# Splitting the first chunk's sixteen weight blocks into twelve and four around the second chunk, in a fused attention and two-layer expert kernel

## The chip, the cores and the metric

One core of one Trainium2 chip runs the whole kernel as one launch. The metric is device time in microseconds. Three runs of the kernel before took 1052.74, 1054.63 and 1058.1 us; their median, 1054.63 us, is the time before. One further execution was recorded by the hardware profiler: it took 1055.97 us, of which 1054.2 us are the span that the profile shows.

## What is computed

The reference has three stages. `a` is 4 numbers, `b` is 2.

```python
# 1: attention over windows: 32 queries against 8 memory rows and 56 context rows
scores = scale * q_c @ k_full.T
a = exp(scores - scores.max(-1)); a = a / (a.sum(-1) + 1e-9)
x = (a @ v_full), laid out as (3072, 512)
# 2: two dense layers with a rational function between them
h = x @ w_in                                   # (3072, 2048)
g = (a[0] + a[1]*h + a[2]*h**2 + a[3]*h**3) / (1 + |b[0]|*|h| + |b[1]|*h**2 + 1e-6)
x = g @ w_out                                  # (3072, 512)
# 3: each token goes to the best of 8 experts, 512 -> 1024 -> 512 with relu between
```

`w_in` and `w_out` arrive as 64-bit floats. TensorE gets no such numbers, so each weight is rebuilt on the chip as a 32-bit float and cut into a high and a low part; each product in stage 2 is three matmuls (high by high, high by low, low by high).

## The kernel before, in words

The 3072 tokens are 24 groups of 128 (attention) and 8 chunks of three groups (stage 2). The 2048 inner columns are 16 weight blocks of 128. Everything is written out by hand, in program order, on in-order queues: TensorE (PE), VectorE (DVE), ScalarE (ACT), GpSimd (POOL) and the DMA queue of SyncE (SP). A stall of one instruction holds back all that stands behind it on its engine.

**The loop** (L1031) has one step n for each pair of chunk and weight block, chunk by chunk: `i, f = divmod(n, 16)`. Step n issues the first product of pair n (`mm1`, L379: 12 matmuls into one of two banks), the elementwise work of pair n-1 on DVE (`el_t` L399 and L395, `el_g` L413 to L415), the cut of pair n-2 (`split`, L422 and L423), and the second product of pair n-3 (`mm2`, L430, L431, L434: 9 matmuls into three accumulator banks). After the sixteenth `mm2` of a chunk, `evac` copies the three banks to SBUF. Around this, lists name for each step what else runs: attention steps (scores L233, `at_pt` L284, values L297, `at_xt` L316), and the routing of a finished chunk (`rt_steps`, seven chunks inside the loop).

**DVE operations from outside** the elementwise work go to a list `side`; `weave` puts one of them behind each of the five elementwise operations, and the rest at the end of the step.

**Weights.** The 32 pieces (16 blocks of each matrix, 512 KB each) are converted while the first chunk runs. A piece is a load on SP's queue into a raw buffer (L608), three DVE operations (L625, L628, L631, the last being the last to read the raw buffer), a cast on ACT (L619) and a subtraction on POOL (L620). Raw buffers, or slots, are used in turn by three pieces. A freed slot is loaded again at the start of the next step. Four pieces are converted ahead of the loop; `RATE` says how many each step converts, two in most of steps 0 to 15.

**Ahead of the loop** the string `SEQ` orders the first three attention groups: `l` loads, `a` scores, `p` and `v` and `x` the rest, `f` empties `side`, `c3` does three conversion operations, `w` starts a load.

**Groups 3 to 8.** `ATT0` gives the steps of groups 3 to 5. Groups 3 and 5 have a buffer for all keys and values; groups 4 and 6 to 8 load keys and values in halves into one buffer each (six steps, with a load between the halves); from group `G2`, 9, two buffers each are used.

**Three PSUM banks** (`XB`) serve attention and routing. `ban` keeps one for the reciprocal of the rational function up to step `NP` and one as the converter's scratch.

`late_consts` (L973) loads the gate weights and a mask at step 17: POOL clears a tile, SP loads it and the mask, and DVE casts the mask (L977).

Of the kernel before, what the change touches and what calls it, by code (L numbers as in the profile page):

```python
# [18 lines left out]
D = 512  # L19
# [22 lines left out]
@with_exitstack  # L42
def build(ctx: ExitStack, tc, q, k, v, w_in, w_out, a, b, w_gate, w1, w2, cst, out):
# [64 lines left out]
    XX = [XX0, XX1]  # L108
    sxh = [cut(xx0, 1024 * i, 512, (4, 128)) for i in range(2)]
    sxl = [cut(xx0, 1024 * i + 512, 512, (4, 128)) for i in range(2)]  # L110
    hh_ = [cut(xx0, 2048, 1024, (8, 128)), cut(xx1, 1024, 1024, (8, 128))]
    hl_ = [cut(xx1, 0, 1024, (8, 128)), cut(xx1, 2048, 1024, (8, 128))]
    WOb = []
# [46 lines left out]
    def kbuf(g, j):  # L160
        return KV[0][:, 0, j] if g in (1, 3, 5) else ks[j] if g < 3 else k2[j] if g >= G2 else kbd

    def vbuf(g, j):
        return KV[0][:, 1, j] if g in (1, 3, 5) else vs[j] if g < 3 else v2[j] if g >= G2 else vbd

# [3 lines left out]
    def xbuf(g):  # L169
        return xsb if g < 3 else pmb[0] if g < 6 else pmb[1]  # L170

# [13 lines left out]
    def ld_all(g, m, eng=nc.sync):  # L185
        src, buf = ((k, kbuf), (v, vbuf))[m]
        if g in (1, 3, 5):
# [38 lines left out]
    def at_score(g, j):  # L226
# [83 lines left out]
    def at_xt(g):  # L310
# [6 lines left out]
        sl = slice(128 * r, 128 * r + 128)  # L317
        xh, xl = XX[i % 2][:, 0, :, sl], XX[i % 2][:, 1, :, sl]
        nc.scalar.copy(out=xh, in_=pt)
# [8 lines left out]
    def attn_steps(g):  # L328
        def score(j):
            at_score(g, j)  # L330
            if j == 1:
                ld_next(g + 1, ld_k)
                if 4 < g + 1 < 24:
                    ld_q(g + 1)
# [5 lines left out]

        if g in (3, 5):
            def scores():
                score(0)
                score(1)
                if g == 3:
                    ld_q(4)
                    ld_all(5, 0)

            def values():
                pv(0)  # L350
                pv(1)
                if g == 3:
                    ld_all(5, 1)

# [18 lines left out]
    def mm1(n):  # L373
        i, f = divmod(n, 16)
        h = HB[n % 2][:, 0:384]
        m = 0
        for kk in range(4):
            for w, x in ((0, 0), (0, 1), (1, 0)):
                nc.tensor.matmul(  # L379
                    h, lhsT=WI[:, f, w, 128 * kk:128 * kk + 128], rhs=XX[i % 2][:, x, kk, :],  # L380
                    start=(m == 0), stop=(m == 11),
# [43 lines left out]
    def mm2(n):  # L425
        f = n % 16
        gh, gl = GG[:, n % 2, 0], GG[:, n % 2, 1]
        for r in range(3):
            sl = slice(128 * r, 128 * r + 128)
            nc.tensor.matmul(ACC[r], lhsT=gh[:, sl], rhs=wo(f, 0), start=(f == 0), stop=False)  # L430
            nc.tensor.matmul(ACC[r], lhsT=gh[:, sl], rhs=wo(f, 1), start=False, stop=False)  # L431
        for r in range(3):
            sl = slice(128 * r, 128 * r + 128)
            nc.tensor.matmul(ACC[r], lhsT=gl[:, sl], rhs=wo(f, 0), start=False, stop=(f == 15))  # L434

    def evac(i):
        for r in range(3):
            if r == 1:
                nc.vector.tensor_copy(out=X2[:, r, 0:D], in_=ACC[r])
            else:  # L440
                nc.scalar.copy(out=X2[:, r, 0:D], in_=ACC[r])

# [9 lines left out]
    def rt_t(i, r, pb, x2t):  # L452
        pt = pb.rearrange("p (a k) -> p a k", a=4)
        for kk in range(4):
            nc.tensor.transpose(pt[:, kk], X2[:, r, 128 * kk:128 * kk + 128], ident)
        nc.scalar.copy(out=x2t, in_=pb)
# [60 lines left out]
    def rt_cols(i):  # L517
        vt = nc.vector
        ch(lambda: vt.tensor_reduce(out=r_gt, in_=r_ex, op=ALU.add, axis=AX.X))
        ch(lambda: vt.tensor_scalar(out=r_gt, in0=r_gt, scalar1=1e-9, scalar2=None, op0=ALU.add))  # L520
        ch(lambda: vt.reciprocal(out=X2[:, :, D:D + 1], in_=r_gt.unsqueeze(2)))

        def toks():
            for r in range(3):
                nc.gpsimd.tensor_scalar(
                    out=X2[:, r, D + 1:D + 2].bitcast(I32), in0=jcol,
                    scalar1=float(128 * (3 * i + r)), scalar2=None, op0=ALU.add,
# [6 lines left out]
    def rt_store(i, r):  # L534
        x = nc.gpsimd.indirect_dma_start(
            out=xs_d,
            out_offset=bass.IndirectOffsetOnAxis(ap=r_di[:, r:r + 1], axis=0),
            in_=X2[:, r],
            in_offset=None,
# [51 lines left out]
    def slot(m):  # L591
        return m if m < 3 else (0, 3, 4)[m % 3]

# [304 lines left out]
    def w_conv():  # L898
        m = done[0]
        if m < len(order):  # L900
            ops, tail = order[m][1](tmp1, scratch[0])
            side.extend(ops)
# [88 lines left out]
    for g in range(23, 2, -1):  # L991
        base = 16 * (g // 3 - 1) + 5 * (g % 3) - (1 if g < G2 else 0)
        for k_, (o, x) in enumerate(attn_steps(g)):
            if g < 6:
                (at if g == 4 and k_ == 1 else at_)(ATT0[g - 3][k_], x)
            else:
                (at_ if g == 6 and not k_ else at)(base + o, x)
    for i in range(NCH - 1):
        for o, x in rt_steps(i):
            at(16 * (i + 1) + 5 + o, x)  # L1000

    for t in (k2[1], v2[1]):
# [252 lines left out]
```

## Time and profile before

| what | value |
|---|---|
| median of three runs | 1054.63 us (1052.74 to 1058.1) |
| profiled execution | 1055.97 us |
| its span | 1054.2 us |
| PE busy | 994.7 us, 94% |
| DVE busy | 691.2 us, 66% |
| ACT busy | 623.5 us, 59% |
| POOL busy | 381.5 us, 36% |

Busy times count an engine's own work. PE's matmuls are pipelined and their ends are modelled, so 94% is no measure of the peak; what counts below is where PE had nothing to run. A timeline row gives start, length, engine, line, operation, what it writes and reads, and in brackets how long the engine had been idle before it and what ended that. The clock column (PEclk) is the granted clock of TensorE as a share of its upper level.

### The profile page before, as it was taken

The numbers are of one execution on the slowest core, as the hardware profiler recorded it, in microseconds if no ns is written. First come the engines' busy times: TensorE is split into PE (matmuls) and PEld (weight loads), VectorE is DVE, ScalarE is ACT, GpSimd is POOL, SyncE is SP. The second block draws the span as 40 slices with busy tenths as digits, with TensorE's granted clock in tenths as the row PEclk, the third lists the DMA queues.
The fourth block names the chain that finished last, engine by engine and source line by source line (L and its number), as shares of the span: only waits on it lengthen the run. The fifth ranks groups of instructions, "written<-read, shape, count | busy, mean of one in ns | idle before, by whom it ended". The sixth has DMA issues, their size and how long they took to land. (4 is left out here: it accounts for less than half of the span.)

```text
span 1054.2 us, 18765 instructions
## 1 busy us (share of the span) xinstructions
PE 994.7 (94%) x6427; PEld 851.1 (81%) x6427; DVE 691.2 (66%) x1276; ACT 623.5 (59%) x1178; POOL 381.5 (36%) x412
## 2 busy tenths in 40 slices
PE   4678879999999999999999999998999999999996
PEld 3566668888888888888888888886888888888885
DVE  5799877767787787787787788967423424344421
ACT  2577567767777777777777778865423324234321
POOL 2367554453363464464464464541100000000010
PEclk9699899999999999999999999999999999999999
DMA  9755422341121121121121022022115133144311
GB/s 245 209 183 167 144 61 71 91 120 52 51 81 51 51 81 51 51 80 51 52 81 51 21 101 70 1 71 70 43 43 198 35 111 131 51 165 156 112 41 38
DMA packets 48460, 93.10 MB, mean 88 GB/s; under 512 B 6999, under 2 KB 15455, under 8 KB 48352
## 3 DMA queue, kind: packets, MB, share of 16 engines
q1 hardware_dynamic: 43520, 78.52, 24.5%
q0 software_dynamic: 4080, 12.61, 3.2%
q8 instruction: 53, 0.87, 0.3%
q10 hardware_dynamic: 752, 0.65, 0.3%
q14 instruction: 55, 0.45, 0.1%
HBM read 169.32 MB, written 15.50 MB: 175 GB/s over the span
## 5 line engine op out<-in xcount | busy, mean ns | idle before, releaser
L379 PE MATMUL bank<-XX,WI 128*128 128x384 f32 x1536 | 303.7, 346 | 7.8 <-DVE EL L395 5.3
L379 PEld LDWEIGHTS bank<-XX,WI 128*128 128x128 f32 x1536 | 270.8, 191 | 20.5 <-DVE EL L395 6.5
L389 POOL TENSOR_TENSOR EL<-EL 128x384 f32<-128x384 f32 x128 | 133.6, 1044 | 235.4 <-ACT EL L388 235.3
L423 POOL TENSOR_TENSOR GG<-EL,GG 128x384 fp32r<-128x384 f32 x128 | 131.9, 1031 | 82.3 <-ACT GG L422 44.2
L777 PE MATMUL bank<-WI,XX 128*128 128x512 f32 x648 | 156.8, 397 | 2.7 <-ACT XX L765 1.5
L777 PEld LDWEIGHTS bank<-WI,XX 128*128 128x128 f32 x648 | 120.5, 190 | 28.3 <-ACT XX L765 1.6
L818 POOL DMA_INDIRECT out_dram<-X,ix x27 | 27.2, 1006 | 298.4 <-DVE ix L817 282.4
L430 PE MATMUL bank<-WOa,GG 128*128 128x512 f32 x288 | 116.4, 404 | 0.0
L431 PE MATMUL bank<-WOa,GG 128*128 128x512 f32 x288 | 115.5, 401 | 0.0
L422 ACT CAST GG<-EL 128x384 fp32r<-128x384 f32 x128 | 65.2, 509 | 72.7 <-DVE EL L415 52.5
L415 DVE SCALAR_TENSOR_TENSOR EL<-EL,ab 128x384 f32<-128x384 f32 x112 | 103.9, 927 | 3.3
L413 DVE SCALAR_TENSOR_TENSOR EL<-EL 128x384 f32<-128x384 f32 x112 | 62.3, 556 | 62.8 <-ACT EL L406 50.1
L387 ACT ACTIVATE EL<-bank 128x384 f32<-128x384 f32 x128 | 62.1, 485 | 67.4 <-PE bank L379 65.8
L794 ACT CAST XX<-bank 128x512 fp32r<-128x512 f32 x54 | 29.1, 592 | 109.2 <-PE bank L792 109.2
L388 ACT ACTIVATE EL<-EL,babs 128x384 f32<-128x384 f32 x128 | 90.8, 709 | 4.3
L766 DVE TENSOR_TENSOR XX<-bank,XX 128x512 fp32r<-128x512 f32 x28 | 19.4, 692 | 108.7 <-ACTq L755 85.0
L784 ACT ACTIVATE EL<-bank 128x512 f32<-128x512 f32 x54 | 29.4, 595 | 100.4 <-PE bank L777 99.2
L801 PE MATMUL bank<-WI,XX 128*128 128x512 f32 x216 | 86.9, 402 | 1.1 <-ACTq L755 0.9
L399 DVE TENSOR_TENSOR EL<-EL,bank 128x384 f32<-128x384 f32 x128 | 70.1, 547 | 25.1 <-ACT EL L390 25.1
L803 PE MATMUL bank<-WI,XX 128*128 128x512 f32 x216 | 84.7, 392 | 0.0
L802 PE MATMUL bank<-WI,XX 128*128 128x512 f32 x216 | 84.3, 390 | 0.3 <-DVEq L755 0.3
L390 ACT ACTIVATE EL<-bank,na 128x384 f32<-128x384 f32 x128 | 83.8, 654 | 0.0
(198 smaller groups left out, 1733.7 us busy)
## 6 DMA issues: line engine op xcount, KB each, us to landing
AT<-in_w_dram SPq DMA_DIRECT2D x164, 512.0 KB
EL<-in_w_dram SPq DMA_DIRECT2D x52, 512.0 KB
AT<-in_k_dram SPq DMA_DIRECT2D x84, 128.0 KB
AT<-in_v_dram SPq DMA_DIRECT2D x80, 128.0 KB
AT<-in_q_dram SPq DMA_DIRECT2D x23, 256.0 KB
AT<-in_w_out_dram SPq DMA_DIRECT2D x11, 512.0 KB
X<-xs_d SPq DMA_DIRECT2D x18, 257.0 KB
AT<-in_w_in_dram SPq DMA_DIRECT2D x8, 512.0 KB
```

Of the source, the lines that this page charges most:

```text
L379: nc.tensor.matmul(h, lhsT=WI[:, f, w, 128 * kk:128 * kk + 128], rhs=XX[i % 2][:, x, kk, :], start=(m == 0), stop=(m == 11),)
L388: nc.scalar.activation(out=y, in_=u, func=AF.Identity, scale=babs[:, 1:2], bias=babs[:, 0:1])
L389: nc.gpsimd.tensor_tensor(out=y, in0=y, in1=u, op=ALU.mult)
L390: nc.scalar.activation(out=t, in_=h, func=AF.Identity, scale=na[:, 3:4], bias=na[:, 2:3])
L415: lambda: vt.scalar_tensor_tensor(out=t, in0=t, scalar=ab[:, 0:1], in1=w, op0=ALU.subtract, op1=ALU.mult),
L423: nc.gpsimd.tensor_tensor(out=gl, in0=g, in1=gh.bitcast(F32), op=ALU.subtract)
L430: nc.tensor.matmul(ACC[r], lhsT=gh[:, sl], rhs=wo(f, 0), start=(f == 0), stop=False)
L431: nc.tensor.matmul(ACC[r], lhsT=gh[:, sl], rhs=wo(f, 1), start=False, stop=False)
L777: nc.tensor.matmul(hbank(j)[c], lhsT=x[:, kk], rhs=w[kk][:, 512 * c:512 * c + 512], start=(kk == 0 and m == 0), stop=(kk == 3 and m == 2),)
L801: nc.tensor.matmul(y, lhsT=hh[:, c], rhs=wh, start=(c == 0), stop=False)
L802: nc.tensor.matmul(y, lhsT=hh[:, c], rhs=wl, start=False, stop=False)
L803: nc.tensor.matmul(y, lhsT=hl[:, c], rhs=wh, start=False, stop=(c == 7))
```

## The change

The pairs get a new order: chunk 0 with blocks 0 to 11, chunk 1 with all 16, chunk 0 with blocks 12 to 15, then chunks 2 to 7 as before. The first twelve blocks' sums of chunk 0 are copied to SBUF after step 14 (in `X2B`, inside the space of raw slots 3 and 4), and the last four blocks' sums are added to them after step 34. Conversion is spread over steps 0 to 22; from piece 24 on, every load uses slot 0. Attention groups 3 to 5 finish by step 11, each with the whole-group buffer; groups 6 to 8 run from step 14, their last part at steps 28 to 30. Because `X2B` overlaps the second buffers, the two-buffer form starts at group 14 instead of 9. Routing of chunk 1 starts at step 33, that of chunk 0 at step 37. Groups 1 and 2 use one subtraction and one exponential instead of eight exponentials with a bias each. The constants are loaded at step 24.

```diff
-G2 = 9
+G2 = 14
 SEQ = (
-    "lq0 lk0 w lq1 lk1 lv1 w a0 lq2 lk2 w f p0 f v0 lv2 c3 w f x0 f a1 lk3 f c2 p1 c1 f v1 lv3 f "
-    "a2 i3 lq3 lk4 w x1 f c3 p2 f v2 i4 lv4 w c2 f x2 n c1 f"
+    "lq0 lk0 w lq1 lk1 lv1 w a0 lq2 lk2 w f p0 f v0 lv2 c3 w a1 lk3 f x0 c2 f p1 a2 i3 lq3 c1 f "
+    "v1 lv3 w p2 f x1 c3 f v2 i4 w c3 f x2 n f"
 )
-RATE = [2, 2, 2, 2, 2, 1, 2, 2, 1, 2, 2, 1, 2, 2, 2, 1]
-NP = 16
-ATT0 = [[0, 1, 2, 3], [4, 5, 6, 7, 8, 9], [10, 11, 12, 13]]
+RATE = [2, 2, 2, 2, 1, 2, 1, 2, 1, 2, 1, 1, 1, 0, 0, 1, 1, 1, 1, 1, 1, 1, 1]
+NP = 14
+SPLIT = 12
+CE = 23
+ATT0 = [
+    [0, 1, 2, 3], [4, 5, 6, 7], [8, 9, 10, 11],
+    [14, 15, 17, 18, 19, 28], [18, 19, 21, 22, 23, 29], [22, 23, 25, 26, 27, 30],
+]
...
+    X2B = cut(AT, 4608, 3 * XW, (3, XW))
...
+    ORD = [(0, f) for f in range(SPLIT)] + [(1, f) for f in range(16)]
+    ORD += [(0, f) for f in range(SPLIT, 16)] + [(i, f) for i in range(2, NCH) for f in range(16)]
...
-        return xsb if g < 3 else pmb[0] if g < 6 else pmb[1]
+        return xsb if g in (0, 1, 2, 7) else pmb[0] if g < 6 else XT if g == 8 else pmb[1]
...
-            if 1 <= g <= 4:
+            if 3 <= g <= 4:
...
-                if 4 < g + 1 < 24:
+                if g + 1 < 24:
                     ld_q(g + 1)
...
     def mm1(n):
-        i, f = divmod(n, 16)
+        i, f = ORD[n]
...
     def mm2(n):
-        f = n % 16
+        i, f = ORD[n]
+        first, stop = (i, f) in ((i, 0), (0, SPLIT)), (i, f) in ((i, 15), (0, SPLIT - 1))
...
-    def evac(i):
+    def evac(i, f):
+        t = x2(i)
         for r in range(3):
-            if r == 1:
-                nc.vector.tensor_copy(out=X2[:, r, 0:D], in_=ACC[r])
+            if (i, f) == (0, 15):
+                nc.vector.tensor_tensor(out=t[:, r, 0:D], in0=ACC[r], in1=t[:, r, 0:D], op=ALU.add)
+            elif r == 1:
+                nc.vector.tensor_copy(out=t[:, r, 0:D], in_=ACC[r])
...
     def slot(m):
-        return m if m < 3 else (0, 3, 4)[m % 3]
+        return m if m < 3 else (0, 3, 4)[m % 3] if m < 2 * SPLIT else 0
...
-    for f in range(16):
-        if f + 3 < 16:
+    for f in range(SPLIT):
+        if f + 3 < SPLIT:
             order.append((0, f + 3))
         order.append((1, f))
+    order += [(0, f) for f in range(SPLIT, 15)] + [(1, SPLIT), (0, 15)] + [(1, f) for f in range(SPLIT + 1, 16)]
...
-    for i in range(NCH - 1):
+    for i in (1, 0, *range(2, NCH - 1)):
         for o, x in rt_steps(i):
-            at(16 * (i + 1) + 5 + o, x)
+            at((37, 33)[i] + o if i < 2 else 16 * (i + 1) + 5 + o, x)
...
-    at(17, late_consts)
+    at(CE + 1, late_consts)
...
-        if n == NP:
+        if n == CE:
             assert done[0] == len(order)
             ban.discard(2)
...
-        if n == 13:
-            assert done[0] <= 28
+        if n == 12:
             switch()
...
-        for _ in range(RATE[n] if n < 16 else 0):
+        for _ in range(RATE[n] if n < CE else 0):
             w_conv()
...
+        if n == SPLIT - 1:
+            flush()
...
-            if (n - LAG) % 16 == 15:
-                evac((n - LAG) // 16)
+            i, f = ORD[n - LAG]
+            if f == 15 or (i, f) == (0, SPLIT - 1):
+                evac(i, f)
```

## Rows read from the trace of the kernel before

**Rows 1.** The page's busy times, and PE's busy tenths in 40 slices.
```profile
PE 994.7 (94%) x6427; PEld 851.1 (81%) x6427; DVE 691.2 (66%) x1276; ACT 623.5 (59%) x1178; POOL 381.5 (36%) x412
...
PE   4678879999999999999999999998999999999996
```

**Rows 2.** Timeline of PE: `mm1` of steps 0, 32 and 33, and what precedes 32.
```profile
36.14 4.25 PE L379 MATMUL bank<-XX,WI 128*128 128x384 f32 x12 [0.67 <-ACT XX L319]
...
231.23 0.60 PE L284 MATMUL bank<-cf,AT 128*128 128x128 f32 x4
231.58 2.35 PE L379 MATMUL bank<-XX,WI 128*128 128x384 f32 x12
235.87 2.24 PE L379 MATMUL bank<-XX,WI 128*128 128x384 f32 x12
```

**Rows 3.** Timeline of DVE: scaling the values of groups 0 and 2, ahead of the loop.
```profile
15.28 0.69 DVE L306 TENSOR_TENSOR AT<-bank,rs 128x512 f32<-128x512 f32 x1 [0.64 <-PE bank L297]
...
33.60 0.69 DVE L306 TENSOR_TENSOR AT<-bank,rs 128x512 f32<-128x512 f32 x1 [1.59 <-PE bank L297]
```

**Rows 4.** Timeline of DVE: first operation of steps 1, 8, 9, 10, 12, 13.
```profile
42.26 0.55 DVE L399 TENSOR_TENSOR EL<-EL,bank 128x384 f32<-128x384 f32 x1
...
91.17 0.55 DVE L399 TENSOR_TENSOR EL<-EL,bank 128x384 f32<-128x384 f32 x1
...
95.53 0.55 DVE L399 TENSOR_TENSOR EL<-EL,bank 128x384 f32<-128x384 f32 x1
...
102.49 0.55 DVE L399 TENSOR_TENSOR EL<-EL,bank 128x384 f32<-128x384 f32 x1
...
114.89 0.54 DVE L399 TENSOR_TENSOR EL<-EL,bank 128x384 f32<-128x384 f32 x1
...
124.98 0.55 DVE L399 TENSOR_TENSOR EL<-EL,bank 128x384 f32<-128x384 f32 x1
```

**Rows 5.** Timeline of DVE and SP, and a window: last reader, reload, end of its traffic.
```profile
128.69 0.68 DVE L631 SCALAR_TENSOR_TENSOR AT<-X,bank 128x512 int32<-128x512 int32 x1
...
129.39 0.33 SPq L608 DMA_DIRECT2D X<-in_w_out_dram  x1
...
132.50:133.00 0.50, 0.50 (x4) 0.42 (x3) 0.50 (x1) 0.49 (x1) 0.00 (x0) 1.00 0.01 0
```

**Rows 6.** Timeline of DVE: a piece's first and last operation, woven into a step.
```profile
133.52 0.69 DVE L625 TENSOR_SCALAR bank<-AT 128x512 int32<-128x512 int32 x1
...
135.64 0.68 DVE L631 SCALAR_TENSOR_TENSOR X<-AT,bank 128x512 int32<-128x512 int32 x1
```

**Rows 7.** Groups by form: L415 with PSUM (60 to 160 us); L423, L415 without (200 to 600).
```profile
L415 DVE SCALAR_TENSOR_TENSOR EL<-EL,ab,bank 128x384 f32<-128x384 f32 x14 | 8.5, 607 | 0.1
...
L423 POOL TENSOR_TENSOR GG<-EL,GG 128x384 fp32r<-128x384 f32 x80 | 81.4, 1018 | 36.0 <-ACT GG L422 27.1 <-DVE r_mx L495 7.3 <-POOL X L525 0.8
...
L415 DVE SCALAR_TENSOR_TENSOR EL<-EL,ab 128x384 f32<-128x384 f32 x81 | 71.7, 886 | 2.3
```

**Rows 8.** Timelines of DVE and PE at the constants of step 17.
```profile
153.13 0.23 DVE L977 CAST upb<-XT 128x128 bf16<-128x128 f32 x1 [5.90 <-DMA XT<-in_cst_dram]
...
154.52 3.09 PE L379 MATMUL bank<-XX,WI 128*128 128x384 f32 x12 [3.23 <-DVE EL L395]
161.03 2.35 PE L379 MATMUL bank<-XX,WI 128*128 128x384 f32 x12
```

**Rows 9.** Timeline of PE where group 8 meets group 9.
```profile
220.23 0.66 PE L297 MATMUL bank<-AT 128*32 128x128 f32 x16 [2.31 <-DMA AT<-in_v_dram]
220.82 3.86 PE L379 MATMUL bank<-XX,WI 128*128 128x384 f32 x12
```

**Rows 10.** Two idle stretches of PE, and the granted clock behind the longer one.
```profile
96.74 0.66 PE L316 MATMUL bank<-cf,AT 128*128 128x128 f32 x4 [1.41 <-DVE AT L306]
...
103.69 1.08 PE L233 MATMUL bank<-KV,AT 128*32 128x128 f32 x32 [2.13 <-DVE XX L320]
...
104.00:108.00 4.00, 4.00 (x38) 3.12 (x29) 4.00 (x8) 1.17 (x3) 2.88 (x3) 0.58 0.86 255
```

More of the change, by code (lines that the diff above doesn't have):

```diff
@@ L108, in build @@
     XX = [XX0, XX1]
[L109 to L112, printed above, removed]
+    sxh = [cut(xx1, 1024 * i, 512, (4, 128)) for i in range(2)]
+    sxl = [cut(xx1, 1024 * i + 512, 512, (4, 128)) for i in range(2)]
+    hh_ = [cut(xx1, 2048, 1024, (8, 128)), cut(xx0, 1024, 1024, (8, 128))]
+    hl_ = [cut(xx0, 0, 1024, (8, 128)), cut(xx0, 2048, 1024, (8, 128))]
+    X2B = cut(AT, 4608, 3 * XW, (3, XW))
     WOb = []
@@ L138, in build, with xx, x2 @@
     c1 = T([128, 1], "c1")
+    ORD = [(0, f) for f in range(SPLIT)] + [(1, f) for f in range(16)]
+    ORD += [(0, f) for f in range(SPLIT, 16)] + [(i, f) for i in range(2, NCH) for f in range(16)]
+    def xx(i):
+        return XX[i if i < 2 else (i + 1) % 2]
+    def x2(i):
+        return X2B if i == 0 else X2
     S = {}
@@ L160, in kbuf @@
     def kbuf(g, j):
-        return KV[0][:, 0, j] if g in (1, 3, 5) else ks[j] if g < 3 else k2[j] if g >= G2 else kbd
+        return KV[0][:, 0, j] if g in (1, 3, 4, 5) else ks[j] if g < 3 else k2[j] if g >= G2 else kbd
     def vbuf(g, j):
-        return KV[0][:, 1, j] if g in (1, 3, 5) else vs[j] if g < 3 else v2[j] if g >= G2 else vbd
+        return KV[0][:, 1, j] if g in (1, 3, 4, 5) else vs[j] if g < 3 else v2[j] if g >= G2 else vbd
     def pbuf(g):
@@ L186, in ld_all @@
         src, buf = ((k, kbuf), (v, vbuf))[m]
-        if g in (1, 3, 5):
+        if g in (1, 3, 4, 5):
             for h in range(2):
@@ L317, in at_xt @@
         sl = slice(128 * r, 128 * r + 128)
-        xh, xl = XX[i % 2][:, 0, :, sl], XX[i % 2][:, 1, :, sl]
+        xh, xl = xx(i)[:, 0, :, sl], xx(i)[:, 1, :, sl]
         nc.scalar.copy(out=xh, in_=pt)
@@ L339, in pv @@
                 ld_next(g + 1, ld_v)
-        if g in (3, 5):
+        if 3 <= g <= 5:
             def scores():
@@ L344, in scores @@
                 score(1)
-                if g == 3:
-                    ld_q(4)
-                    ld_all(5, 0)
+                if g < 5:
+                    ld_all(g + 1, 0)
             def values():
@@ L351, in values @@
                 pv(1)
-                if g == 3:
-                    ld_all(5, 1)
+                if g < 5:
+                    ld_all(g + 1, 1)
             return [(0, scores), (1, lambda: at_pt(g)), (2, values), (3, lambda: at_xt(g))]
@@ L429, in mm2 @@
             sl = slice(128 * r, 128 * r + 128)
-            nc.tensor.matmul(ACC[r], lhsT=gh[:, sl], rhs=wo(f, 0), start=(f == 0), stop=False)
+            nc.tensor.matmul(ACC[r], lhsT=gh[:, sl], rhs=wo(f, 0), start=first, stop=False)
             nc.tensor.matmul(ACC[r], lhsT=gh[:, sl], rhs=wo(f, 1), start=False, stop=False)
@@ L433, in mm2 @@
             sl = slice(128 * r, 128 * r + 128)
-            nc.tensor.matmul(ACC[r], lhsT=gl[:, sl], rhs=wo(f, 0), start=False, stop=(f == 15))
-    def evac(i):
+            nc.tensor.matmul(ACC[r], lhsT=gl[:, sl], rhs=wo(f, 0), start=False, stop=stop)
+    def evac(i, f):
+        t = x2(i)
         for r in range(3):
-            if r == 1:
-                nc.vector.tensor_copy(out=X2[:, r, 0:D], in_=ACC[r])
+            if (i, f) == (0, 15):
+                nc.vector.tensor_tensor(out=t[:, r, 0:D], in0=ACC[r], in1=t[:, r, 0:D], op=ALU.add)
+            elif r == 1:
+                nc.vector.tensor_copy(out=t[:, r, 0:D], in_=ACC[r])
             else:
-                nc.scalar.copy(out=X2[:, r, 0:D], in_=ACC[r])
+                nc.scalar.copy(out=t[:, r, 0:D], in_=ACC[r])
     L = T([128, 3, E], "L")
@@ L454, in rt_t @@
         for kk in range(4):
[L455 removed]
+            nc.tensor.transpose(pt[:, kk], x2(i)[:, r, 128 * kk:128 * kk + 128], ident)
         nc.scalar.copy(out=x2t, in_=pb)
@@ L520, in rt_cols @@
         ch(lambda: vt.tensor_scalar(out=r_gt, in0=r_gt, scalar1=1e-9, scalar2=None, op0=ALU.add))
-        ch(lambda: vt.reciprocal(out=X2[:, :, D:D + 1], in_=r_gt.unsqueeze(2)))
+        ch(lambda: vt.reciprocal(out=x2(i)[:, :, D:D + 1], in_=r_gt.unsqueeze(2)))
         def toks():
@@ L525, in toks @@
                 nc.gpsimd.tensor_scalar(
-                    out=X2[:, r, D + 1:D + 2].bitcast(I32), in0=jcol,
+                    out=x2(i)[:, r, D + 1:D + 2].bitcast(I32), in0=jcol,
                     scalar1=float(128 * (3 * i + r)), scalar2=None, op0=ALU.add,
@@ L537, in rt_store @@
             out_offset=bass.IndirectOffsetOnAxis(ap=r_di[:, r:r + 1], axis=0),
-            in_=X2[:, r],
+            in_=x2(i)[:, r],
             in_offset=None,
@@ L900, in w_conv @@
         if m < len(order):
-            ops, tail = order[m][1](tmp1, scratch[0])
+            ops, tail = order[m][1](tmp1 if m < 2 * SPLIT else tmp1[0:2], scratch[0])
             side.extend(ops)
@@ L993, in build @@
         for k_, (o, x) in enumerate(attn_steps(g)):
-            if g < 6:
-                (at if g == 4 and k_ == 1 else at_)(ATT0[g - 3][k_], x)
-            else:
-                (at_ if g == 6 and not k_ else at)(base + o, x)
-    for i in range(NCH - 1):
+            if g < 9:
+                (at_ if g < 6 else at)(ATT0[g - 3][k_], x)
+            else:
+                at(base + o, x)
+    for i in (1, 0, *range(2, NCH - 1)):
         for o, x in rt_steps(i):
-            at(16 * (i + 1) + 5 + o, x)
+            at((37, 33)[i] + o if i < 2 else 16 * (i + 1) + 5 + o, x)
     for t in (k2[1], v2[1]):
-        at(20, lambda t=t: nc.gpsimd.memset(t[64:128, 0], 0.0))
-        at(21, lambda t=t: nc.gpsimd.memset(t[0:64, 1], 0.0))
+        at(49, lambda t=t: nc.gpsimd.memset(t[64:128, 0], 0.0))
+        at(50, lambda t=t: nc.gpsimd.memset(t[0:64, 1], 0.0))
     zsrc = vbd[64:128, 0].rearrange("p a k -> p (a k)")
```

2 lines of the change are left out of this document (1 added, 1 removed).

## The prediction

> **What bounds the kernel now.** The page comes first: PE is busy for 94% of the span, and the slices show where it isn't, namely in the first six (some 160 us) and in the last [rows 1]. From there to the expert stage PE has no gap that counts, so the end of the kernel moves by what PE gains or loses ahead of it. The timeline of PE gives the two ends of that stretch: `mm1` of step 0 starts at 36.14, that of step 32, the first of chunk 2, at 231.58; later a step takes 4.29 us [rows 2], so 32 of them would be 137 us of 195. The timeline of DVE says why: its steps are full. A step with one piece takes 4.36 us (91.17 to 95.53), one with two pieces and one attention operation 6.96 us (95.53 to 102.49); with 0.6 us for the attention operation a second piece costs 2.0 us [rows 4]. So DVE sets the pace of steps 1 to 15, and PE waits for it.
>
> I book the change as the shift of `mm1` of step 32, plus what PE still has to do behind it.
>
> **Ahead of the loop.** The new order puts group 1's scores ahead of group 0's last part, and groups 1 and 2 do one subtraction on DVE and one exponential in place of eight. From the scaling of group 0's values (15.28 us) to that of group 2's, DVE then has 20 operations of 0.69 us, some 0.72 apart: 9 of conversion, 6 of maximum, subtraction and sum, 3 scalings, 2 low parts. With 0.8 us of short ones and 1.2 us of waiting for the scores of group 1 it ends at 31.7 us. Before, that scaling ended at 33.60 + 0.69 = 34.29 [rows 3], 1.85 us ahead of `mm1` of step 0 [rows 2]. **-2.6 us**; bounds 0 (if loads aren't there in time, since three groups and four pieces are wanted sooner) and -4.
>
> **Steps 1 to 12.** They convert 18 pieces where they converted 21: 3 x 2.0 = 6.0 us less on DVE. Group 5 now finishes inside them, two operations more: +1.2. Step 12 took 10.09 us (114.89 to 124.98) [rows 4], where two pieces and group 5's sum come to 7.3; PE was waiting there for the exponentials of group 5, with too little conversion to fill the time. The same stage now falls in step 9, which has two pieces: I take 2.3 of the 2.8 us back. **-7.1 us**; bounds -4.8 and -8. Step 13 then starts on DVE at 124.98 - 2.6 - 7.1 = 115.3 instead of 124.98.
>
> **Steps 13 to 23.** Steps 13 and 14 convert nothing and go at PE's pace: 8.3 us. The first copy of the sums (two on ACT, one on DVE) lies under PE's next `mm1`. In step 15 DVE has 5.9 us up to the end of its piece: 129.5. From here each step converts one piece, and every piece uses slot 0. The reload stands on SP behind L631 of the piece before, and L625 of the next piece stands in DVE's queue behind the first operation of the step; all elementwise work behind it waits too, and PE waits for that, as its next `mm1` needs the bank that L395 frees. The nearest rows give the price: L631 ended at 129.37, the load was issued at 129.39, its traffic was over by 132.50 [rows 5]: 3.2 us with the signal. L625 to the end of L631, woven, is 133.52 to 136.32, 2.8 us [rows 6]. A round takes 6.1 us with the hand-over, and that holds for four of the seven steps 16 to 22. In the other three, attention operations stand ahead of the piece in `side` and push L631 to the end of the step; counted at the pitch of the rows they come to 7.4, 8.0 and 7.4. Together 47.2 us; end of the last piece 176.7, with the rest of step 22 (1.4) 178.1. Bounds: 38.8 if loads never hold DVE (its own operations alone), and 64 if PE runs these seven steps at its lower clock.
>
> Steps 15 to 23 also take the reciprocal from SBUF, because `NP` comes two steps earlier: L415 takes 886 ns on average without a PSUM operand and 607 ns with one [rows 7]. The 0.28 us is in the counts above; where DVE waits for a load it costs nothing. The Trainium skill (SBUF — State Buffer, Who interferes with whom) says that a DVE operation with two SBUF inputs and a GpSimd operation that reads SBUF exclude each other for a whole instruction. By that, each of the five steps in which DVE doesn't wait could lose a whole POOL subtraction of 1.02 us [rows 7] instead of 0.28: 3.7 us more in the sum. I keep the mean, since 81 such operations, next to the same POOL work, lost no more.
>
> Step 23 has no piece but three attention operations: 4.7 us, to 182.8.
>
> **The constants, step 24.** Moved with all they issue: POOL's clear, two loads on SP, the cast on DVE. The cast kept DVE idle for 5.90 us at step 17 and PE for 3.23 us; the `mm1` behind it took 3.09 us and the next came 6.5 us later [rows 8]. Nothing in the change shortens the chain (ACT's cast, POOL's cut and clear, SP's loads of some 2.8 us), but POOL has no weight piece in front of it: I take 4.5. The cast comes at 187.3, `mm1` of step 25 at 188.7 (153.13 to 154.52 is 1.39), step 26 at 195.2. Six steps of 4.29 and 2.85 us of attention (half a group's values, three last parts of 0.35 us, two half scores; 16 such small matmuls are 0.59 us, 220.23 to 220.82 [rows 9]) bring `mm1` of step 32 to 223.7, against 231.58. From the start of step 13 that is 108.4 us against 106.6: **+1.8 us**, bounds -7 and +18. The shift of step 32 is -2.6 - 7.1 + 1.8 = -7.9.
>
> **What PE still has to do then.** The routing of chunk 0 now lies behind step 32: 15 transposes (four take 0.35 us, 231.23 to 231.58 [rows 2]), 24 small matmuls, and the ranks, some 2.4 us, and the transposes of group 9, 0.35: **+2.75 us**. The second sums are added by three DVE operations (2.1 us) at step 34, in DVE's idle time; without that cover they would delay the next accumulation by as much. Before, group 9 with its two buffers put five loads on SP ahead of group 8's last values, and PE waited for 2.31 us, with 1.5 us more for the slow `mm1` behind [rows 9]. Group 8 loses that wait (the 231.58 includes it), but the first group with two buffers is now 14, next to 13, with the same loads in the same order: **+3.8 us**, bounds 0 and 3.8. Groups 9 to 13 have a load between their halves, queued on SP behind the scores of the next group; in groups 6 to 8, with PE full, no other such wait counts, so **0**, bounds 0 and +5, since two routings now share three banks, and PE may wait for one.
>
> **Sum:** -7.9 + 2.75 + 3.8 = -1.35 us. The profiled execution took 1055.97, so 1054.6; it was 1.3 us above the median, so the forecast is 1053.3 us. About 0.5% (5.3 us) is what a measurement of this kernel can tell from no change.
>
> **Rivals.** *DVE isn't held by slot 0.* If SP's reload lands before the next L625, steps 16 to 22 cost 38.8 instead of 47.2 us: 1044.9. For it: DVE still has L414, L415 and L399 to do in the meantime, some 1.7 us. Against it: 3.2 us is longer than that. A start of the loop that gains 4 us, and no wait at group 14, would reach 1048 together; these carry the faster side too. *PE falls to its lower clock in steps 15 to 23.* The place is the wait in front of each `mm1`, 2 us in steps that wait for a load and nearly 3 in the others. After 1.41 us of idleness the clock stayed, after 2.13 us the next stretch ran at 0.58 [rows 10], between the levels of 1.2 and 2.4 GHz; the point lies between, and this kernel is on it. If PE stays at the lower level, a step is twice 4.29 plus attention, 9.1 us, and seven take 64: 1070. Against it: a slow `mm1` fills the gap that caused it, so the fall would end itself. *The single-buffer groups 9 to 13 wait as rows 9 show*, at each of their four meetings: 4 x 3.8 = 15 us, 1068.5; it decides where SP is over 2 us late with the half, and only the meeting with five loads was. That the change does nothing can't be: the order is fixed in the program.
>
> **Chances.** The forecast, within 0.5%: 0.46. Faster by more: 0.34, mostly the first rival. Slower by more: 0.20, of which 0.11 for the clock, 0.09 for groups 9 to 13. The range, 1045 to 1062, reaches to the first rival and halfway to the others, which leaves out about 2 in 10; the unknown waits at slot 0 alone span most of it.
>
> **What would show it.** In the new profile: `mm1` of step 0 near 33.5 us; step 13 near 115; in steps 16 to 22 L625 idle for a DMA, some 1.5 us in four of them, steps of 6 to 8 us; the cast of the constants idle 4 to 6 us; from about 190 us PE full, and a wait near 2.3 us where group 13 meets 14. I am wrong if L625 never waits there, if PE's clock stays low for tens of us, or if PE shows gaps between 230 and 330 us.

## The result, and the profile after

The changed kernel takes **1070.41 us** (median of four runs, 1066.93 to 1072.57), the kernel before 1054.87 beside it (four runs): a ratio of 1.0142, interval 1.0104 to 1.0179. It is slower by 1.4%, where the forecast was 1053.3. The traced execution is the quickest of the four, 1066.93 us with a span of 1065.1; against 1055.97 and 1054.2 before, the two traces differ by 10.9 us of span, and the medians by 15.5. The 4.6 in between are the places of the two traced executions among their runs: the one after is 3.5 below its median, the one before 1.1 above. The sums below go by the traces.

The page of the changed kernel, busy times, PE's slices and its clock:

```profile
PE 997.7 (94%) x6427; PEld 852.2 (80%) x6427; DVE 693.6 (65%) x1281; ACT 620.3 (58%) x1148; POOL 383.8 (36%) x412
...
PE   4668977899999999999999999999999999999996
...
PEclk8689998899999999999999999999999999999999
```

PE has as many matmuls as before [rows 1]; of the 10.9 us, 7.9 are idle time of PE and 3.0 longer busy time. Slices six to eight (some 133 to 213 us) now hold a 7, a 7 and an 8, where they held a 7, a 9 and a 9. The timeline of PE has the same two marks as [rows 2], `mm1` of steps 0 and 32:

```profile
34.79 4.61 PE L393 MATMUL bank<-XX,WI 128*128 128x384 f32 x12 [0.68 <-ACT XX L334]
...
236.14 2.35 PE L393 MATMUL bank<-XX,WI 128*128 128x384 f32 x12
```

The start gained 1.35 us (36.14 to 34.79); step 32 is 4.56 later (231.58 to 236.14). DVE's first operation of a step (L413 now, L399 in [rows 4]) and its long waits say where the difference arose. The rows are steps 1, 6 (its wait alone), 13, 16, then the waits of L643 in steps 16, 18, 20 and 22, then step 23 and the cast of the constants:

```profile
41.26 0.56 DVE L413 TENSOR_TENSOR EL<-EL,bank 128x384 f32<-128x384 f32 x1 [1.50 <-ACT EL L404]
...
81.19 0.55 DVE L427 SCALAR_TENSOR_TENSOR EL<-EL,bank 128x384 f32<-128x384 f32 x1 [3.32 <-ACT bank L420]
...
122.07 0.55 DVE L413 TENSOR_TENSOR EL<-EL,bank 128x384 f32<-128x384 f32 x1
...
137.39 0.54 DVE L413 TENSOR_TENSOR EL<-EL,bank 128x384 f32<-128x384 f32 x1
141.22 0.69 DVE L643 TENSOR_SCALAR bank<-X 128x512 int32<-128x512 int32 x1 [3.29 <-DMA X<-in_w_in_dram]
...
155.64 0.69 DVE L643 TENSOR_SCALAR bank<-X 128x512 int32<-128x512 int32 x1 [3.78 <-DMA X<-in_w_out_dram]
...
171.19 0.69 DVE L643 TENSOR_SCALAR bank<-X 128x512 int32<-128x512 int32 x1 [3.63 <-DMA X<-in_w_out_dram]
...
185.40 0.69 DVE L643 TENSOR_SCALAR bank<-X 128x512 int32<-128x512 int32 x1 [3.57 <-DMA X<-in_w_out_dram]
...
189.39 0.55 DVE L413 TENSOR_TENSOR EL<-EL,bank 128x384 f32<-128x384 f32 x1
...
199.55 0.23 DVE L996 CAST upb<-XT 128x128 bf16<-128x128 f32 x1 [5.07 <-DMA XT<-in_cst_dram]
```

Steps 16 to 22 take 52.0 us (137.39 to 189.39), and in four of the seven the first operation of the piece (L643, L625 before) waits for slot 0, 14.3 us together. PE stands behind it. The four longest waits of PE in this stretch and up to the constants:

```profile
156.38 1.08 PE L248 MATMUL bank<-AT 128*32 128x128 f32 x16 [4.06 <-DMA AT<-in_k_dram]
...
172.45 4.21 PE L393 MATMUL bank<-XX,WI 128*128 128x384 f32 x12 [4.39 <-DVE EL L409]
...
186.27 0.65 PE L248 MATMUL bank<-AT 128*32 128x128 f32 x16 [2.00 <-DMA AT<-in_k_dram]
...
200.95 3.84 PE L393 MATMUL bank<-XX,WI 128*128 128x384 f32 x12 [2.55 <-DVE EL L409]
```

Two of the four are put down to keys, not to slot 0. SP's queue shows why (start, length, the load it issues):

```profile
151.43 0.34 SPq L626 DMA_DIRECT2D X<-in_w_out_dram  x1
151.86 0.47 SPq L191 DMA_DIRECT2D AT<-in_k_dram  x1
```

The keys are queued behind a reload that waits for DVE to have read slot 0 (151.43), and so land late for PE's scores at 156.38. Whether that order costs anything by itself is an experiment below. The window of this stretch, with PE's busy time first and its granted clock third from the end:

```profile
137.00:189.00 52.00, 39.53 (x281) 33.26 (x280) 36.29 (x66) 27.69 (x52) 23.78 (x21) 0.88 0.42 120
```

PE is busy for 39.5 of 52 us. The clock is 0.88 on average, and the `mm1` behind the waits of 4.39 and 2.55 take 4.21 and 3.84 us where one at the upper level takes 2.35: the slower clock follows the waits.

Behind step 32 two marks carry on: DVE's first operation of step 32, and its copy of the last sums of chunk 7. First the kernel before, then the changed one:

```profile
231.16 0.55 DVE L399 TENSOR_TENSOR EL<-EL,bank 128x384 f32<-128x384 f32 x1 [0.34 <-ACT EL L390]
...
708.52 0.69 DVE L439 COPY X<-bank 128x512 f32<-128x512 f32 x1 [4.64 <-PE bank L434]
```
```profile
235.40 0.56 DVE L413 TENSOR_TENSOR EL<-EL,bank 128x384 f32<-128x384 f32 x1 [0.63 <-ACT EL L404]
...
720.78 0.69 DVE L457 COPY X<-bank 128x512 f32<-128x512 f32 x1 [4.63 <-PE bank L449]
```

From step 32 to the end of stage 2 it was 477.4 us and is 485.4: 8.0 more (7.7 from `mm1` of step 32, which starts 0.74 behind DVE's first operation now and 0.42 before). The expert stage is 1.4 shorter. So 4.56 + 7.70 - 1.36 = 10.9, the difference of the spans.

### The profile page after: what moved, and what is told of

Read it like the earlier page. It is cut to its first block, busy times and chain, and to the rows that moved or that the text cites. A ratio compares the mean times of both kernels' runs of the same rounds, so it can differ in the third digit from the quotient of the medians.

```text
span 1065.1 us, 18719 instructions
## 1 busy us (share of the span) xinstructions
PE 997.7 (94%) x6427; PEld 852.2 (80%) x6427; DVE 693.6 (65%) x1281; ACT 620.3 (58%) x1148; POOL 383.8 (36%) x412
## 5 line engine op out<-in xcount | busy, mean ns | idle before, releaser
L393 PE MATMUL bank<-XX,WI 128*128 128x384 f32 x1536 | 307.8, 349 | 11.6 <-DVE EL L409 10.1
L393 PEld LDWEIGHTS bank<-XX,WI 128*128 128x128 f32 x1536 | 273.8, 194 | 25.5 <-DVE EL L409 12.3
L403 POOL TENSOR_TENSOR EL<-EL 128x384 f32<-128x384 f32 x128 | 133.1, 1040 | 235.6 <-ACT EL L402 234.1
L836 POOL DMA_INDIRECT out_dram<-X,ix x27 | 29.4, 1089 | 294.8 <-DVE ix L835 278.8
L429 DVE SCALAR_TENSOR_TENSOR EL<-EL,ab 128x384 f32<-128x384 f32 x114 | 101.6, 891 | 3.3
L427 DVE SCALAR_TENSOR_TENSOR EL<-EL 128x384 f32<-128x384 f32 x114 | 63.3, 556 | 53.8 <-ACT EL L420 41.6
L413 DVE TENSOR_TENSOR EL<-EL,bank 128x384 f32<-128x384 f32 x128 | 70.1, 547 | 24.9 <-ACT EL L404 24.9
```

What stands on the lines that cost most here:

```text
L393: nc.tensor.matmul(h, lhsT=WI[:, f, w, 128 * kk:128 * kk + 128], rhs=xx(i)[:, x, kk, :], start=(m == 0), stop=(m == 11),)
L403: nc.gpsimd.tensor_tensor(out=y, in0=y, in1=u, op=ALU.mult)
L429: lambda: vt.scalar_tensor_tensor(out=t, in0=t, scalar=ab[:, 0:1], in1=w, op0=ALU.subtract, op1=ALU.mult),
```

## The experiments

My theory after the result: slot 0 sets steps 16 to 22, as a round of conversion and reload that is longer than a step, and what goes on behind step 32 is a fixed price of splitting the chunk. The rivals: the order of SP's queue, the exponentials, the clock, the start.

**No reload.** From piece 25 on nothing is loaded; the conversion reads what lies in slot 0.

```diff
-            order[loaded[0]][0]()
+            if loaded[0] <= 2 * SPLIT:
+                order[loaded[0]][0]()
```

> The changed kernel, but weight pieces 25 to 31 are not loaded: their conversion reads what lies in slot 0, and the last four weight blocks are wrong. Theory (the reload of slot 0 holds DVE): the four idle stretches in front of the first conversion operation in steps 16, 18, 20 and 22 (14.3 us in the changed kernel's profile) go; steps 16 to 22 take about 39 us instead of 52, and the median falls by 11 to 14 us, to 1057 to 1059. Rival (the conversion itself is too much work for DVE beside the second chunk, whatever the loads do): steps 16 to 22 stay above 47 us and the median above 1065.

The part on stage 2 came out: no wait of L643 is left, and steps 16 to 22 take 40.6 us (DVE's L413, steps 16 and 23):

```profile
137.95 0.54 DVE L413 TENSOR_TENSOR EL<-EL,bank 128x384 f32<-128x384 f32 x1
...
178.53 0.55 DVE L413 TENSOR_TENSOR EL<-EL,bank 128x384 f32<-128x384 f32 x1
```

11.4 us less than 52.0, and the copy of chunk 7's sums comes at 710.66 instead of 720.78. The expected median was missed (1082.39, ratio 1.0259, 1.0232 to 1.0286): with other weights the tokens go to other experts, and the stage behind took 369.0 us (1079.7 - 710.66) instead of 344.3, with 120 matmuls more (6547 in all, 6427 before). I should have seen that and named stage 2 alone.

**Attention loads ahead of the reload.** From step 13 on SP issues the loads of a step's attention operations first.

```diff
-        for m in freed:
-            nxt(m)
-        freed.clear()
+        if n < 13:
+            for m in freed:
+                nxt(m)
+            freed.clear()
...
         for x in todo.pop(n, []):
             x()
+        for m in freed:
+            nxt(m)
+        freed.clear()
```

> The changed kernel, but from step 13 on SP issues the loads of a step's attention operations ahead of the reload of slot 0, where they stood behind it. Theory (slot 0's own round of conversion and reload sets steps 16 to 22; the attention halves stuck behind it add two waits of PE that DVE's wait would have caused anyway): PE's waits for keys at 156.38 and 186.27 (4.06 and 2.00) shrink to under 1; DVE's waits in the first operation of a piece stay, together 12 to 17 (14.3 before); S(16) to S(23) stays within 4 of 52.0; median 1066 to 1072. Rival (SP's order is what costs, and slot 0 only because a load that waits blocks the queue): the waits of DVE go below 6 together, and the median falls by over 5, to under 1065.

1070.76 us, ratio 1.0149 (1.0119 to 1.018): the same time, as expected. PE's waits for keys are gone, and the waits of L643 have grown:

```profile
140.59 0.69 DVE L643 TENSOR_SCALAR bank<-X 128x512 int32<-128x512 int32 x1 [3.31 <-DMA X<-in_w_in_dram]
...
155.15 0.69 DVE L643 TENSOR_SCALAR bank<-X 128x512 int32<-128x512 int32 x1 [3.90 <-DMA X<-in_w_out_dram]
...
170.27 0.69 DVE L643 TENSOR_SCALAR bank<-X 128x512 int32<-128x512 int32 x1 [3.39 <-DMA X<-in_w_out_dram]
...
186.93 0.69 DVE L643 TENSOR_SCALAR bank<-X 128x512 int32<-128x512 int32 x1 [6.01 <-DMA X<-in_w_out_dram]
```

16.6 us together. The keys that stood in line behind the reload were a symptom; slot 0's round is the bound of these steps.

**The last eight pieces every second step.** First with the odd steps:

```diff
-RATE = [2, 2, 2, 2, 1, 2, 1, 2, 1, 2, 1, 1, 1, 0, 0, 1, 1, 1, 1, 1, 1, 1, 1]
-CE = 23
+RATE = [2, 2, 2, 2, 1, 2, 1, 2, 1, 2, 1, 1, 1, 1, 0, 1, 0, 1, 0, 1, 0, 1, 0, 1, 0, 1, 0, 1]
+CE = 28
...
-    at(CE + 1, late_consts)
+    at(24, late_consts)
```

> The changed kernel with the last eight pieces converted in steps 13, 15, ... 27 instead of 15 to 22, all still through slot 0; constants stay at step 24. Theory (reload holds DVE): a reload now has over one whole step without a piece, no wait for it over 1 us is left, and the median falls by 8 to 12 us, to 1058 to 1062. Rival (the number of pieces counts, not their distance): the same work is only spread further, up to step 27, and the median stays within 3 us of 1070.

1062.05 us, ratio 1.0066 (1.0045 to 1.0087), at the upper edge of what was expected. L643 waits no more, but the reload now stands on SP ahead of the attention halves of the odd steps, and PE waits for them: 2.65 us at step 19 and 1.84 at step 23 for keys, 2.43 near 203 for values; the constants wait 6.72. So the order on SP does count as soon as slot 0 isn't the bound.

Then with the even steps 14 to 28, whose loads come a step away from the halves; the conversion's result goes to the one buffer that nobody reads then (`tmp1[1:2]`), `CE` is 29.

```diff
+RATE = [2, 2, 2, 2, 1, 2, 1, 2, 1, 2, 1, 1, 1, 0, 1, 0, 1, 0, 1, 0, 1, 0, 1, 0, 1, 0, 1, 0, 1]
```

> As the spread kernel, but with the last eight pieces in the even steps 14, 16, ... 28, so that a reload stands on SP in odd steps, where no half of a group's keys or values is wanted in the next step; the value buffer of these pieces is always the same one. Theory (in the spread kernel PE waited some 2 us each in steps 19, 23 and 27 because the halves stood on SP behind a reload that waits for the step's last DVE operation): those three waits go, the third sums of chunk 7 come 5 to 8 us earlier than in the spread kernel (713.9 us), and the median is 1055 to 1058. Rival (those waits come from DMA traffic of the reload itself, not from its place on SP): the waits stay, within 2 us of the spread kernel's 1062.

**1053.8 us**, ratio 0.9984 (0.9966 to 1.0002): 16.6 less than the change as it was by the medians, 13.8 by the spans of the two traces (1065.1 and 1051.3), more than expected, and level with the kernel before. Neither DVE nor PE waits for slot 0 or for a half. The same stretch as above, in this kernel's window:

```profile
137.00:189.00 52.00, 48.55 (x344) 42.20 (x343) 44.74 (x78) 35.75 (x68) 27.15 (x26) 0.97 0.43 119
```

PE has 48.6 us of work in it instead of 39.5, and its clock is at 0.97 with no other edit. That speaks against the clock as a cause. The reloads themselves are all still there, so their traffic isn't it either.

**One exponential for groups 3 and 4 as well.**

```diff
-            if 3 <= g <= 4:
+            if False:
```

> The changed kernel, with groups 3 and 4 too in the form with one subtraction and one exponential. Theory (PE waited 4.8 us and DVE 3.3 us in step 6 because group 4's eight exponentials stand behind the casts in ACT's queue and the transposes now follow in the next step): DVE's wait in step 6 falls to under 1 us and the median by 2 to 4 us, to about 1067. Rival (the wait is that of any attention step placed one step behind its scores; group 5, with one exponential, cost PE 3.2 us as well): the wait stays near 3 us and the median within 1 us of 1070.4, since DVE gets two operations more per group.

1067.05 us, ratio 1.0104 (1.0077 to 1.0132): 3.4 less than the change by the medians, with intervals that overlap. The wait of 3.32 us in step 6 is gone, so its cause is shown; what that is worth is not. Steps 1 to 12 take 78.85 us instead of 80.81, but 80.08 and 81.12 in two later traces with this edit, and 78.38 to 81.24 in five traces without it: on average 80.0 and 80.3. For each of the two groups DVE gets two operations of 0.68 us in place of one of 0.27, as the rival said in the main. Eight short exponentials with their read-outs had held ACT from 73.28 to 75.76; PE waited 4.77 us for them at 75.81, and DVE's L427 for the reciprocal that ACT does behind.

**The start alone, in the kernel before.** `SEQ` of the change with group 4's loads kept, and one exponential for groups 1 and 2:

```diff
-            if 1 <= g <= 4:
+            if 3 <= g <= 4:
```

> The kernel before with only the new order ahead of the loop (loads of group 4 kept in it, and one exponential for groups 1 and 2). Theory: this part is worth what the changed kernel's start showed, 1.35 us at mm1 of step 0 (34.79 against 36.14), so that the median falls by 1 to 2 us, to 1053 to 1054. Rival one, the prediction's term: 2.6 us. Rival two: nothing, because the next steps wait for weight loads and DVE takes the time back.

1054.66 us, ratio 0.999 (0.9974 to 1.0005), above what was expected. `mm1` of step 0 comes at 35.67 instead of 36.14, and chunk 7's sums 1.3 us earlier: at most about a microsecond, which neither the median nor one trace can tell from nothing.

**G2 = 14 alone, in the kernel before.**

```diff
-G2 = 9
+G2 = 14
```

> The kernel before with one edit: the two-buffer form starts at group 14 instead of 9. Theory of the prediction (groups with one buffer cost nothing where PE is full, and the wait between groups 8 and 9 moves to 13 and 14): 1054.9 within 1.5 us. Rival (one-buffer groups and the two routings in steps 32 to 50 cost PE; the changed kernel lost 3 us more than forecast there, and this edit alone holds the first half of it): 2 to 4 us slower, 1057 to 1059.

1055.31 us, ratio 0.9998 (0.9982 to 1.0014): the median that the theory gave, but not by its mechanism. It gains ahead of step 32 (3.2 us in steps 30 and 31), where groups 8 and 9 no longer meet [rows 9], and gives it back behind: from DVE's first operation of step 32 (226.34 instead of 231.16) to the copy at 708.17 it takes 481.8 us instead of 477.4. Of these 4.5, 0.8 stand ahead of chunk 1's copy and 2.1 in chunk 2's window, with the one-buffer groups, and 1.65 in chunk 3's, where groups 13 and 14 meet (80.11 between the copies of two chunks, against 78.46). PE doesn't wait in chunk 2's window; it runs 16 more score matmuls there, and two halves take 0.64 us each where a whole group's 32 matmuls take 1.08. That explains a part; the rest wasn't followed.

**The cast of the constants two steps behind its load, in the kernel before.**

```diff
+    def late_cast():
         nc.vector.tensor_copy(out=upb, in_=XT[:, 0:128])
...
+    at(19, late_cast)
```

> The kernel before with one edit: the cast of the constants comes at step 19, two steps behind their load. Theory: DVE's 5.9 us and PE's 3.2 us of waiting at step 17 go, with the slow mm1 behind them: 3 to 5 us faster, 1050 to 1052. Rival (PE then waits as long for the late attention loads of steps 16 to 19): within 1.5 us of 1054.9.

1050.67 us, ratio 0.9957 (0.9942 to 0.9973), as expected. The 5.90 us of [rows 8] were not the constants' price but that of a cast too early in DVE's queue.

**Group 8's second half first, in that kernel.** Group 9's next loads go one step later.

```diff
+        if g == G2:
+            return [
+                (-3, lambda: (at_score(g, 0), at_score(g, 1))),
+                (-2, lambda: (ld_next(g + 1, ld_k), ld_q(g + 1))),
...
```

> The kernel before with the cast of the constants two steps behind their load (1050.67 by itself), and with group 9's next loads one step later, so that the second half of group 8's values goes first on SP. Theory (the half stands behind five loads): the wait of 2.9 at that meeting and the slow first product behind it go, which were some 3.8 together, median 1046.5 to 1048. Rival (the wait is for the bank or moves to group 9's own halves): within 1.5 of 1050.67. Chance of the first 0.6.

1046.97 us, ratio 0.9924 (0.9904 to 0.9944): 3.7 less by the medians, as expected. By the traces step 30 takes 4.94 us instead of 7.31, so 2.4 less, which is the wait alone. PE's rows at that meeting, without this edit and with it:

```profile
214.01 0.64 PE L297 MATMUL bank<-AT 128*32 128x128 f32 x16 [2.29 <-DMA AT<-in_v_dram]
214.59 2.35 PE L379 MATMUL bank<-XX,WI 128*128 128x384 f32 x12
```
```profile
214.78 0.65 PE L297 MATMUL bank<-AT 128*32 128x128 f32 x16
```

In [rows 9] the `mm1` behind the same wait took 3.86 us, here 2.35: the slow one, some 1.5 us, is not in every execution.

**All mends in the changed kernel.** First the even steps, one exponential for all groups and the cast at step 26, two behind the load:

> The even-step kernel with one exponential for groups 3 and 4, and with the cast of the constants two steps behind their load (step 26) instead of right behind it. Theory: the three causes add up; the wait of 5 us for the constants goes (PE loses 2.5 us and a slow mm1 there), step 6 loses its 3.3 us: third sums of chunk 7 at 700 to 704 us, median 1046 to 1051, faster than the kernel before. Rival (what is taken away in one place is waited for in the next): not below 1054.

1050.25 us, ratio 0.9952 (0.9933 to 0.9971), as expected. Then group 14's next loads one step later too, as above:

```diff
+                (-2, lambda: (at_score(g, 0), at_score(g, 1))),
+                (-1, lambda: (ld_next(g + 1, ld_k), ld_q(g + 1))),
```

> The changed kernel with every mend: pieces at the even steps, one exponential, the cast of the constants two steps behind its load, and group 14's next loads one step later so that the second half of group 13's values goes first. Theory (the split itself is worth nothing once its faults are mended, since it pays 2 for one-buffer groups and 2.6 for a second routing): the wait of 0.9 at the 13/14 meeting goes, 1 to 2 less than the 1050.25 without that last edit, median 1048 to 1050, not below the kernel before with the same two mends (1046.97). Rival (the split pays, and its gain was only hidden): median below 1046.

1049.36 us, ratio 0.9939 (0.992 to 0.9958): as expected. The meeting was worth 0.9, by the medians as by chunk 3's window in the traces (79.38 instead of 80.25).

**The start, added to the kernel before with its two mends.** The edits of three runs above together:

> The kernel before with the cast two steps behind its load, group 9's next loads one step later, and the change's new order ahead of the loop with one exponential for groups 1 and 2. By the run of that order alone (0.0 to -1.3): median 1045.5 to 1047 (1046.97 without it), the best of all. Rival: the start is set by the loads and nothing changes, 1046.5 to 1048.

**1044.84 us**, ratio 0.9895 (0.9874 to 0.9916), the best version, 0.7 better than expected. The two kernels, with the same mends but for the one exponential of groups 3 and 4, differ by 4.5 us. DVE's first operation of step 32 and the copy of chunk 7's sums, first with the chunk split, then without:

```profile
219.64 0.55 DVE L421 TENSOR_TENSOR EL<-EL,bank 128x384 f32<-128x384 f32 x1 [0.62 <-ACT EL L412]
...
704.07 0.69 DVE L465 COPY X<-bank 128x512 f32<-128x512 f32 x1 [4.64 <-PE bank L457]
```
```profile
222.40 0.55 DVE L407 TENSOR_TENSOR EL<-EL,bank 128x384 f32<-128x384 f32 x1 [0.34 <-ACT EL L398]
...
699.73 0.69 DVE L447 COPY X<-bank 128x512 f32<-128x512 f32 x1 [4.64 <-PE bank L442]
```

The split is 2.8 us ahead at step 32 (1.3 of them already at step 1) and pays 7.1 behind it (484.4 against 477.3). One wait in it was left as it is, 3.62 us of PE at step 28, where the last piece and a last part of attention need the same step:

```profile
203.88 0.65 PE L331 MATMUL bank<-cf,AT 128*128 128x128 f32 x4 [3.62 <-DVE X L657]
```

Without it the two might come near to each other; that wasn't tried.

## Why the prediction was wrong, point by point

Its sum was -7.9 for step 32, +6.55 behind, together -1.35; the traces say +4.56, +7.70 and -1.36 (the expert stage, which it left at 0). The second half came near; the first half missed by 12.5 us.

- **Start**, -2.6 forecast: -1.35, and -0.5 for the order by itself. It took 1.2 us of waiting in DVE's chain; the trace has 4.25, and the scaling of group 2's values ended at 32.94, not 31.7. The start differs between traces of the same code: 33.80 to 36.54 in eight with the change's start (mean 35.2), 36.14 to 37.00 in four with the old one (mean 36.7).
- **Steps 1 to 12**, -7.1 forecast, measured -1.9 (DVE, step 1 to step 13: 82.7 before, 80.8 now). This is the step that failed most, by 5.2. Traces with these steps in common spread, but none is near the forecast: 80.73 to 83.39 in four of the kernel before's form (mean 81.9), 78.38 to 81.24 in five of the change's (mean 80.3), so -1.6 on average. The work was counted rightly: without its waits from step 1 on DVE has 77.2 us before (waits of 5.5) and 72.3 now (8.5), 4.9 less, and 6.0 - 1.2 was 4.8. But the waits rose by 3.0 where 2.3 were taken back. In their place PE's and ACT's chain of scores, exponentials and transposes came to the front: 3.32 at group 4's exponentials (step 6), as the run with one exponential shows, 1.38 for group 5 (step 11). The price of a wait that goes was counted, and that DVE would be waiting elsewhere wasn't.
- **Steps 13 to 15**: 1.1 more than forecast. Steps 13 and 14, which convert nothing, took 9.6 us and not 8.3.
- **Steps 16 to 22**, the round of slot 0: the mechanism was the one forecast, four visible waits, but each was mis-sized. A reload took 3.7 to 4.2 us, from its issue to the L643 that it releases (137.50 to 141.22, 151.43 to 155.64), where 3.2 were taken, from the end of its traffic [rows 5]. Four of them, 0.8 longer on average, are 3.2 us; DVE's first operation of step 23 came 52.0 behind that of step 16 instead of 48.6. The idle time forecast in front of L625, 1.5 us, was off by more, 3.3 to 3.8: it took three operations of DVE to lie under the reload, but in the steps ahead of these four L649 stands right before the next step's first operation (136.79 and 137.39), and only that one does. The rival "not held by slot 0" has its price nearly right: 38.8 to the end of the last piece, 40.2 with the 1.4 behind it, and 40.6 measured without the reload. So the price of slot 0, 8.4 in the prediction, was 11.4 in this stretch. The even steps gain 13.8 by the traces, but they also leave only four of the seven pieces in these steps.
- **L415 without a PSUM operand**: the mean was kept, but it is the mean of two values. Its successor L429 takes 0.62 us in the steps 16, 18, 20 and 22, and 0.91, 0.86, 1.05, 0.86 and 1.26 in the five in which DVE doesn't wait (15, 17, 19, 21, 23). The long ones started while a subtraction or product ran on POOL, and each ended 0.41 to 0.43 us behind its end, as did one L428 of 1.33 us among others of 0.55. The rows of step 23, DVE and POOL:

```profile
193.23 1.26 DVE L429 SCALAR_TENSOR_TENSOR EL<-EL,ab 128x384 f32<-128x384 f32 x1
...
193.03 1.04 POOL L403 TENSOR_TENSOR EL<-EL 128x384 f32<-128x384 f32 x1 [1.80 <-ACT EL L402]
```

  So the rule in the Trainium skill (SBUF — State Buffer, Who interferes with whom) can be seen in all five: DVE loses the rest of POOL's instruction. Together with the L428 that is 2.6 us beyond 0.62 and 0.55, where the mean gave 1.4 and a whole instruction each time 5.1.
- **The constants**: a wait of 5.07 and 2.55 of PE's, forecast 4.5 as a whole; that stretch missed by 1.0. That no chain need wait there, since a cast may stand two steps later, was not seen.
- **Behind step 32**: 2.75 + 3.8 + 0 = 6.55 against 7.7, near in sum by two errors, which is luck. The meeting at group 14 lies in a window that is 1.65 to 1.9 longer, of which 0.9 went with the mend, not 3.8 (PE's wait was 0.91 us, at 366.44), and the one-buffer groups 9 to 13, taken as 0, cost up to 2.9 by the run of `G2` alone (0.8 ahead of chunk 1's copy, 2.1 behind it). What is left, 8.0 - 4.5 = 3.5, is the second routing for the most part, forecast as 2.75 with group 9's transposes. From step 32 to chunk 2's copy it can be read off, first `G2` alone, then the change:

```profile
226.34:320.76 94.42, 94.42 (x685) 81.31 (x683) 71.23 (x135) 70.55 (x133) 45.71 (x51) 1.00 0.22 65
```
```profile
235.40:333.06 97.66, 97.31 (x733) 83.69 (x731) 74.45 (x151) 71.88 (x136) 50.92 (x63) 1.00 0.23 69
```

  PE runs 48 instructions more, all of them the routing's by the groups of lines, and takes 3.2 us longer.
- **The rivals.** The clock fell, to 0.88 on average in the stretch, but as a consequence: with the reloads spread it was 0.97. That the median lies at this rival's 1070 is chance; its seven steps were to take 64 us and took 52. That 2.13 us of idleness bring the clock down was read from one trace; in another the same 2.13 us didn't (last section). Groups 9 to 13 cost up to 2.9 us and not 15, without a wait of PE in chunk 2's window. The outcome is no rival's; it is the forecast's own mechanism, with three terms of its sum mis-sized (steps 1 to 12, the rounds, the start).

By the traces the forecast for the traced execution was 1054.6 and came out 12.3 us higher: 5.2 from steps 1 to 12, 3.4 from the rounds, 1.6 from the start as DVE saw it at step 1, 1.1 and 1.0 from steps 13 to 15 and the constants, and the rest is within a microsecond.

## What to carry to other kernels

A load into a buffer that was just read is priced from its issue to the first instruction that it releases, not to the end of its traffic, and a single buffer in use every step costs the whole round of load and conversion. Here its use in every second step hid that at no cost in buffers, once no load that is wanted sooner stood behind the reload. When work is taken from the engine that sets the pace, list its waits of before and of after with the work, since the chain next in line keeps part of the gain. And where a change gathers several edits, mend the kernel before with the same edits first: here the mends and the new start were worth 1% without the split, and the split, as far as it was mended, brought nothing on top.

## What the runs showed of the hardware

- A reload of 512 KB released a waiting DVE 3.7 us after its issue when alone and 4.0 to 4.2 with other transfers queued behind it. The lone one was issued at 137.50; its traffic was over by 140.80 (DMA share 0.00 in the window below), and L643 started at 141.22, 0.4 us behind that:

```profile
137.50 0.38 SPq L626 DMA_DIRECT2D X<-in_w_in_dram  x1
...
140.80:141.20 0.40, 0.00 (x0) 0.00 (x0) 0.00 (x0) 0.00 (x0) 0.38 (x1) 1.00 0.00 0
```

  The Trainium skill (DMA: Bandwidth & Descriptors, Anatomy of one DMA — SWDGE (gpsimd) path) gives 2.0 us plus the bytes at 436 GB/s for GpSimd's path, an estimate of 3.2 us for this size; SP's rows here are above it.
- An engine's wait may name the wrong culprit of a pair: PE waited 4.06 us for keys that only stood behind a waiting reload on SP, and issuing them first changed the time by nothing (1070.76 against 1070.41).
- TensorE came back to a granted clock of 0.97 in a stretch of 52 us as soon as the waits in it were gone (0.88 with them).
- The same wait of PE came out both ways. In the kernel before the granted clock was 0.50 behind 2.13 us of idleness (104.69 to 106.69), and 0.63 and 0.58 behind 2.31 (220.20 to 222.20, 222.20 to 224.50). In the kernel with the later cast it was 1.00 behind 2.13 (103.94) and behind 2.29 (214.01), with the same work around. So the length of a wait alone didn't say whether the slow `mm1` comes.
- Over the whole trace of the change, 44 of the 114 rows of L429 start while POOL runs a tensor operation. All 44 end 0.40 to 0.43 us behind its end, with a mean of 1.28 us; of the other 70, 68 take 0.62. It holds the other way round too: a POOL L403 that started 0.08 us behind an L429 (206.06, 0.62 us) took 1.41 us instead of some 1.02.
